# Gradient row operands made inside the last attention, dW2 stored there between zeros, and two-bank output tiles from the attention's end

## The chip, the cores and the metric

The kernel runs on one core of one Trainium2 chip. The metric is the device time of one execution in microseconds (us), lower is better. A time is quoted as the median of the runs of one kernel, with the lowest and highest in brackets. A profile is of one of those executions; its span is about 2 us shorter than the time of the same run. In the profile PE is the matmul engine, PEld its weight load, DVE, ACT and POOL the vector, scalar and general engines, SP the engine that here only issues transfers (SPq is its queue). L222 is a line of the kernel.

The program uses one core, so there is no second die to compare with. A run counts as slow when it is over 1.5% above the fastest of the same kernel.

## The reference, cut to what matters

One token goes through two identical layers (attention, then a Mish MLP) that share their weights, and the function returns the output and the gradients of everything.

```python
def _A_ref(x, k_cache, v_cache, wq, wo):      # D=1024, 32 query heads, 4 KV heads, Dh=128
    W = 4096                                  # a window at the end of a cache of Sk=32768
    q = (x @ wq).reshape(B, 1, 32, 128).transpose(0, 2, 1, 3)
    k = repeat(k_cache[:, :, Sk - W:], 8);  v = repeat(v_cache[:, :, Sk - W:], 8)
    p = softmax(einsum("bhqd,bhkd->bhqk", q, k) * Dh ** -0.5)
    return einsum("bhqk,bhkd->bhqd", p, v).reshape(B, 1, 4096) @ wo
def _B_ref(x, w1, b1, w2):                    # F=3584
    h = x @ w1 + b1
    return (h * tanh(softplus(h))) @ w2
def f(x, ...):
    x = x + _A_ref(_layernorm(x), ...); x = x + _B_ref(_layernorm(x), ...)
    x = x + _A_ref(_layernorm(x), ...); x = x + _B_ref(_layernorm(x), ...)
    return x
out, vjp = jax.vjp(f, x, k_cache, v_cache, wq, wo, w1, b1, w2)
return out, *vjp(grad_out)                    # y, dx, dK, dV, dWq, dWo, dW1, db1, dW2
```

Two things follow. The gradients of the shared weights are sums of two outer products, one per layer, so each is a matrix of rank 2: almost no arithmetic and much to store. And 7/8 of dK and dV are zeros, because only the window of the cache is read: 58.7 MB of zeros, stored as 112 transfers of 0.524 MB from one tile of zeros. These zero stores need no data, so the kernel may issue them at any time. They are the only work of which this is true. The profile gives 98.58 MB written to HBM and 72.89 MB read.

## The kernel before

The backward pass runs from the last layer to the first. The last big thing on it is the backward of the first layer's attention ("the last attention"): it streams wo in (the "wo stream"), forms the gradient of the softmax, multiplies by K, and then goes through the 32 heads with wq (the "dn loop", because it forms the gradient dn of the layer norm's output). After it come one layer norm and the outputs that are left: the last stage.

Zero stores are issued either from SP's queue (`zeros`) or from POOL's queue behind a small copy that waits for given data (`bg_zeros`). The table `Z` says how many at which point:

```python
def zeros(n):
    for _ in range(min(n, len(zero_jobs))):
        nc.sync.dma_start(zero_jobs.pop(0), zt[:])
def bg_zeros(n, after):
    if n:
        nc.gpsimd.tensor_copy(gate_t[:], after[:, 0:1])
    for _ in range(min(n, len(zero_jobs))):
        nc.gpsimd.dma_start(zero_jobs.pop(0), zt[:])
# A1c: at the start of the last attention.  A1d: in its middle.  end: behind its layer norm.
Z = dict(B2=3, A3=16, B4=[5, 2, 1, 2, 1, 2, 6], A3c=6, A3d=29, W1=3, A1c=6, A1d=26, end=4)
```

An output is a "job": four matmuls into PSUM, their evictions into a staging tile, one store of 0.524 MB (0.459 MB for dW1). A dK or dV job ("chunk") is stored only with its neighbours, after every fourth chunk; they are staged in the two halves of K's tile, which the prediction calls K halves. The operands of the matmuls are rows, made in "pieces": POOL copies columns into a tile of zeros, PE transposes eight blocks, one engine evicts.

```python
def spread_rows(n, put, dst):                       # one piece
    ...                                             # POOL: put() into a spread tile
    if "pair" in pools: ps = shaped(pools["pair"].tile([P, 2048], BF16, name="rw", tag="pair"), [P, 8, P])
    else:               ps = psum1([P, 8, P], BF16, "rw")
    for j in range(n):
        nc.tensor.transpose(ps[:, j, :], sp[:, j, :], ident_bf[:])
    evac(dst, ps[:, 0:n, :].rearrange("p j x -> p (j x)"), 0.69, 1.0)

def out_banks():                                    # PSUM for one job
    if "pair" in pools:                             # two tiles of two banks, 1024 columns an eviction
        ts = [pools["pair"].tile([P, 1024], FP32, name="ops", tag="pair") for _ in range(2)]
        return [t[:, k * 512:(k + 1) * 512] for t in ts for k in range(2)], [(0, 2, ts[0][:]), (2, 2, ts[1][:])]
    bs = [psum1([P, 512], FP32, "ops") for _ in range(4)]        # four tiles of one bank
    return bs, [(k, 1, bs[k]) for k in range(4)]
```

`psum1` takes one of only four one-bank buffers; the other four banks hold accumulators and, in the attention, two "halves" buffers. The end of the kernel, with cuts:

```python
# in the last attention
bg_zeros(Z["A1c"], g_bf)                            # the start, while the wo stream waits for its loads
...
zeros(Z["A1d"])                                     # behind the wo stream
...
after_v()                                           # V is read: its space becomes rows, spread and staging tiles
...
for h in range(HQ):                                 # the dn loop
    for half in range(2): row_mm(nrow, ...)         # 128*32 columns, 128x512 rows
    if h % 8 == 7: run(1)                           # one dW2 job every 8 heads (two more ran before the loop)
...
# after the last layer norm
bg_zeros(Z["end"], g0b)
rows_put(R["w1"], 0, "nB", "rep"); rows_put(R["w1"], 1, "dh", "pieces")
do3 = row_layout(...); do1 = row_layout(...); tall_left("wo", "o", 0); ...   # all other row operands
run(1000)                                           # 8 dW2 jobs and
dw_wide(lambda: R["w1"], 256, F // 2, True, out_6); run(4)       # 4 dW1 jobs in one-bank tiles
pools["pair"] = ...                                 # from here two-bank tiles
run(1000)                                           # 12 dW1
dkv(sA3["p"], do3, sA1["p"], do1, out_3); ...       # dV, dWo, dK, dWq
```

## Time and profile before

The time before is 459.68 us (458.19 to 460.98, 3 runs). The page's second part cuts the span into 40 slices of 11.5 us. The two rows shown are the busy share of the DMA engines in tenths and what they moved:

```profile
DMA  8999999988999999999998999999995889799997
GB/s 322 387 411 414 406 408 342 410 307 316 416 417 370 390 342 351 411 414 416 416 414 326 311 336 368 359 412 418 416 418 235 354 321 400 309 413 402 418 411 303
```

From slice 27 on (298 us and later) the DMA is the limit: slices at 412 to 418 GB/s, and a few below. The slices 31 to 35 are the ones below. Windows of 10 us show them better. Each row gives the window, its length, the busy time and count of each engine, the clock, the DMA share and GB/s:

```profile
core 0: us, PE busy (x) PEld busy (x) DVE busy (x) ACT busy (x) POOL busy (x), PEclk, DMA share, GB/s
300.00:310.00 10.00, 6.36 (x116) 4.34 (x108) 5.39 (x10) 6.36 (x7) 0.40 (x1) 0.96 1.02 411
330.00:340.00 10.00, 9.26 (x79) 2.14 (x77) 6.46 (x12) 3.01 (x6) 0.00 (x0) 0.58 1.03 417
350.00:360.00 10.00, 6.80 (x49) 4.19 (x47) 7.54 (x23) 4.36 (x6) 5.42 (x28) 0.50 0.63 253
360.00:370.00 10.00, 8.50 (x29) 1.73 (x26) 7.90 (x12) 8.50 (x15) 0.00 (x0) 0.50 0.82 329
370.00:380.00 10.00, 6.33 (x32) 1.31 (x31) 7.60 (x13) 8.46 (x11) 0.00 (x0) 0.50 0.80 319
390.00:400.00 10.00, 7.74 (x66) 2.12 (x62) 10.00 (x10) 9.46 (x10) 0.00 (x0) 0.84 0.73 292
```

A full window has a share of 1.02 or 1.03. The timeline (start, duration, engine, line, operation, output from inputs; in brackets how long the engine idled before it and for what) says what happens in the first low one:

```profile
346.51 0.17 DVE L309 CAST gX_pair<-g_A 128x8 bf16<-128x8 f32 x1
...
349.54 1.89 PE L887 MATMUL rw<-ident_bf,spread 128*128 128x128 bf16 x16 [1.75 <-POOL spread L897]
...
355.47 0.58 ACT L149 CAST wo_b<-ops 128x512 bf16<-128x512 f32 x1 [0.89 <-PE ops L223]
...
357.51 0.33 SPq L974 DMA_DIRECT2D out_dram<-wo_b  x1
```

The last layer norm ends at 346.5. Then the pieces are made, the first output is evicted at 355.5, and its store is issued at 357.5. The DMA lives on what was queued before and on four zeros.

In 300 to 310 the DMA is full although nothing is stored that was computed there. The DMA view of 300 to 304 us, by queue, says what fills it: the software queue, which here carries the six zeros of `A1c`.

```profile
q0 software_dynamic: 433, 1.59, 98.2%
q1 hardware_dynamic: 19, 0.05, 3.4%
```

To add such holes up I took windows of 1 us and summed `1 - share/1.025`, where positive, with 1.025 as the share of a full window. This gives 13.1 us of lost DMA time between 294 and 442 us. It is a sum worked out from the profile, and the rest of the document uses it.

### The profile page before, as it was taken

How to read it: one execution, taken by the hardware profiler on the slowest of the kernel's cores; microseconds unless marked ns; L12 is line 12 of the kernel's file. 1: busy time of each engine (PE TensorE's matmuls, PEld its weight loads, DVE VectorE, ACT ScalarE, POOL GpSimd, SP SyncE). 2: the span in 40 equal slices, each digit the busy share in tenths (PEclk: the TensorE clock that was granted, in tenths of full speed). 3: DMA queues.
4: the chain of work that ended last, by engine and by line, in shares of the span. 5: the costliest groups of instructions: out<-in, count | busy, mean ns of one | idle time of the engine just before them, and what ended most of it. 6: DMA issues, size and time to landing. Idle time of an engine off the chain costs nothing.

```text
span 458.9 us, 11945 instructions
## 1 busy us (share of the span) xinstructions
PE 328.7 (72%) x5080; PEld 225.6 (49%) x5080; DVE 246.9 (54%) x519; ACT 219.3 (48%) x268; POOL 61.5 (13%) x159
## 2 busy tenths in 40 slices
PE   0565755577996998877997889775885676779730
PEld 0333434566466997854895779643534111222100
DVE  3124101376332776663265755564555779999960
ACT  1122100165242886773581655351031689998940
POOL 2000000002422214142330020112006000000000
PEclk9989555596777999895697769987565555755555
DMA  8999999988999999999998999999995889799997
GB/s 322 387 411 414 406 408 342 410 307 316 416 417 370 390 342 351 411 414 416 416 414 326 311 336 368 359 412 418 416 418 235 354 321 400 309 413 402 418 411 303
DMA packets 52257, 172.24 MB, mean 375 GB/s; under 512 B 5200, under 2 KB 12396, under 8 KB 51180
## 3 DMA queue, kind: packets, MB, share of 16 engines
q1 hardware_dynamic: 39680, 126.37, 71.3%
q0 software_dynamic: 12480, 45.11, 24.5%
q8 instruction: 39, 0.64, 0.5%
q14 instruction: 14, 0.11, 0.1%
q10 hardware_dynamic: 44, 0.01, 0.0%
HBM read 72.89 MB, written 98.58 MB: 374 GB/s over the span
## 4 chain that ended last, share of the span: by engine, by line
PE 21%; issue 9%; DVE 8%; ACT 8%; DMA 7%; POOL 1%; DVEq 0%; ACTq 0%; SPq 0%; POOLq 0%
PE tps L187 6%; PE ops L223 5%; DMA w_c<-in_B_w_dram 4%; PE acc L223 4%; ACT wo_b L149 3%; DVE wq_b L146 3%; DMA wo_c<-in_A_wo_dram 3%; DVE K L146 3%; ACT st_o L149 2%; PE d L223 2%; PE tps L602 1%; PE sm L223 1%; PE rw L887 1%; ACT wo_c L149 1%; ACT w_c L603 1%
## 5 line engine op out<-in xcount | busy, mean ns | idle before, releaser
L139 POOL DMA_DIRECT2D out_dram<-zt x86 | 45.7, 535 | 43.3 <-DMA out_dram<-zt 40.7
L223 PEld LDWEIGHTS <-w_c 128*128 128x128 bf16 x1120 | 36.3, 102 | 20.9 <-DMA w_c<-in_B_w_dram 13.9
L603 ACT COPY w_c<-tps 128x1024 bf16<-128x1024 bf16 x28 | 28.3, 1012 | 25.5 <-PE tps L602 24.8
L146 DVE CAST wo_b<-ops 128x512 bf16<-128x512 f32 (+3 forms) x40 | 33.2, 878 | 9.2 <-PE ops L223 8.9
L605 DVE CUSTOM_DVE_ANT_0 scr<-w_c,gbc 128x1024 bf16<-128x1024 bf16 x28 | 34.2, 1221 | 7.2 <-DMA w_c<-in_B_w_dram 5.2
L149 ACT CAST wo_b<-ops 128x512 bf16<-128x512 f32 (+2 forms) x34 | 27.0, 870 | 16.4 <-PE ops L223 16.4
L149 ACT COPY K<-tps 128x1024 bf16<-128x1024 bf16 x19 | 18.7, 1019 | 30.9 <-PE tps L187 30.9
L223 PE MATMUL q<-wq_b,nA_pair 128*32 128x512 bf16 x128 | 14.0, 541 | 16.6 <-DMA wq_b<-in_A_wq_dram 15.1
L770 DVE CUSTOM_DVE_ANT_0 wo_c<-wo_c,gbc 128x1024 bf16<-128x1024 bf16 x14 | 16.3, 1218 | 12.4 <-DMA wo_c<-in_A_wo_dram 10.4
L602 PE MATMUL tps<-ident_bf,w_c 128*128 128x128 bf16 x224 | 22.7, 263 | 0.0
L146 DVE COPY K<-tps 128x1024 bf16<-128x1024 bf16 x13 | 8.8, 689 | 24.9 <-PE tps L187 24.9
L149 ACT COPY w_b<-tps 128x1024 bf16<-128x1024 bf16 x20 | 19.5, 1015 | 5.3 <-PE tps L187 5.2
L187 PE MATMUL tps<-ident_bf,K 128*128 128x128 bf16 x256 | 21.7, 249 | 0.0
L223 PE MATMUL ops<-Tw 2*128 2x512 bf16 x56 | 15.9, 560 | 6.5 <-ACT wo_b L149 4.1
L187 PEld LDWEIGHTS <-K 128*128 128x128 bf16 x256 | 18.4, 114 | 4.1 <-issue 4.0
L223 PE MATMUL acc<-a_pair,w_c 128*128 128x16 bf16 x448 | 16.0, 172 | 5.2 <-DMA w_c<-in_B_w_dram 4.2
L187 PE MATMUL tps<-ident_bf,w_c 128*128 128x128 bf16 x224 | 17.3, 238 | 1.6 <-DMA w_c<-in_B_w_dram 1.6
L146 DVE CAST K<-ops 128x1024 bf16<-128x1024 f32 x15 | 17.7, 1221 | 0.9 <-PE ops L223 0.6
L149 ACT CAST K<-ops 128x1024 bf16<-128x1024 f32 x17 | 17.0, 1012 | 1.7 <-PE ops L223 1.2
L149 ACT COPY w_c<-tps 128x768 bf16<-128x768 bf16 (+1 forms) x14 | 11.6, 829 | 12.6 <-PE tps L187 11.4
L149 ACT COPY wq_b<-tps 128x1024 bf16<-128x1024 bf16 x16 | 15.1, 1054 | 5.1 <-PE tps L187 5.1
L223 PE MATMUL ops<-R 2*128 2x512 bf16 (+1 forms) x64 | 12.3, 544 | 7.0 <-ACT wo_b L149 5.4
(333 smaller groups left out, 684.5 us busy)
## 6 DMA issues: line engine op xcount, KB each, us to landing
out_dram<-zt POOLq DMA_DIRECT2D x86, 512.0 KB, 10.0
wo_c<-in_A_wo_dram SPq DMA_DIRECT2D x28, 512.0 KB, 8.2
w_c<-in_B_w_dram SPq DMA_DIRECT2D x32, 448.0 KB, 5.9
w_c<-in_B_w_dram SPq DMA_DIRECT2D x28, 512.0 KB, 7.0
out_dram<-zt SPq DMA_DIRECT2D x26, 512.0 KB, 8.2
out_dram<-wo_b SPq DMA_DIRECT2D x18, 512.0 KB, 9.1
wq_b<-in_A_wq_dram SPq DMA_DIRECT2D x16, 512.0 KB, 11.8
out_dram<-K SPq DMA_DIRECT2D x8, 1024.0 KB, 8.4
```

The lines of the kernel that those rows point to most:

```text
L139: nc.gpsimd.dma_start(zero_jobs.pop(0), zt[:])
L146: nc.vector.tensor_copy(out_ap, in_ap)
L149: nc.scalar.copy(out_ap, in_ap)
L187: nc.tensor.transpose(ps[:, b, :], ap, ident_bf[:])
L223: nc.tensor.matmul(out_ap, lhsT=lhsT, rhs=rhs, start=start, stop=stop, skip_group_check=True, **kw)
L602: nc.tensor.transpose(ps[:, b, :], w[:, 1, b * P:(b + 1) * P], ident_bf[:])
L603: nc.scalar.copy(w[:, 1, :], ps[:].rearrange("p b c -> p (b c)"))
L605: nc.vector.tensor_tensor_reduce(out=scr[:], in0=w[:, 0, :], in1=gbc[:], scale=1.0, scalar=0.0, op0=ALU.mult, op1=ALU.add, accum_out=wg[:, ...
L770: nc.vector.tensor_tensor_reduce(out=w[:, 0, :], in0=w[:, 0, :], in1=gbc[:], scale=1.0, scalar=0.0, op0=ALU.mult, op1=ALU.add, accum_out=w ...
L887: nc.tensor.transpose(ps[:, j, :], sp[:, j, :], ident_bf[:])
```

## The change

It has three parts. (a) The row operands are made inside the last attention, in the space of wo (free once its rows have been used) and of V, so nothing has to be made after the layer norm. (b) All outputs after the attention use two-bank tiles. (c) dW2 jobs run inside the attention, each behind one zero store, ten in place of six; to have zeros for that, and for between the later outputs, 22 of the zeros that stood at the attention's start and middle are taken from there. The diff is shortened: some lines are joined, and the comments are added here.

```diff
@@ last attention, wo stream
+        if not first:
+            after_do()                              # spread tiles, T, R and staging inside wo_b; dW2 and dW1 jobs
+            prep.extend([...])      # dW2's left rows (2) and right rows, dW1's two sides, do3, q3, db1
         def T(i): ...
+            if not first and i: nextprep()          # one piece for each late wo chunk
@@ behind the wo stream
+            after_stream()
             zeros(Z["A1d"])
@@ softmax gradient
         else:
             after_v()
+            early(2)
-            tall_left("w2", "a", 0)
+            nextprep(1)
...
@@ dn loop
-            run(2)
+            prep.extend([...])      # 7 pieces: dWo's left rows (2) and right rows, dWq's two sides, do1, q1
         for h in range(HQ): ...
-            if not first and h % 8 == 7:
-                run(1)
+            if not first and h % 4 == 3:
+                nextprep()
+                early(1)
@@
+    def early(n):
+        for _ in range(n):
+            zeros(1)
+            run(1)
-    Z = dict(B2=3, A3=16, B4=[5, 2, 1, 2, 1, 2, 6], A3c=6, A3d=29, W1=3, A1c=6, A1d=26, end=4)
+    Z = dict(B2=3, A3=16, B4=[5, 2, 1, 2, 1, 2, 6], A3c=6, A3d=29, W1=3, A1c=0, A1d=10)
@@ last stage
-    R["w1"] = new_rows("R1"); rows_put(R["w1"], ...); do3 = row_layout(...) ...    # all pieces
-    bg_zeros(Z["end"], g0b)
     pacc.release()
-    run(1000)
-    dw_wide(lambda: R["w1"], 256, F // 2, True, out_6)
-    run(4)
     pt.release()
     pools["pair"] = ...
...
+    while jobs:
+        run(7)
+        zeros(1)
+    zeros(1000)
```

More of the change, by code (lines that the diff above doesn't have):

```diff
@@ L70 @@
     strm = ctx.enter_context(tc.tile_pool(name="strm", bufs=NB))
-    vpool = tc.alloc_tile_pool(name="vpool", bufs=1)
     pt = tc.alloc_tile_pool(name="pt", bufs=4, space=bass.MemoryType.PSUM)
@@ L374, in pipe @@
                 M(items[i - lag], i - lag)
+    area = {}
     def row_layout(col32, name):
-        x = pools["rows"].tile([P, G, DH], BF16, name=name, bufs=1)
+        x = area[name].rearrange("p (g d) -> p g d", g=G)
         ps = psum1([P, P], BF16, "rps")
@@ L381, in row_layout @@
             nc.vector.tensor_scalar(out=x[:, g, :], in0=ps[:, 0:P], scalar1=gmask[:, g:g + 1], scalar2=None, op0=ALU.mult)
-        return x
     def pad_tile(name):
@@ L426, in attn_fwd @@
                     nc.sync.dma_start(wq_t[2 * t + hf], wq_v[:, t, hf * (J // 2):(hf + 1) * (J // 2)])
-            load_kv(vpool, "V", v_v)
+            load_kv(keep, "V", v_v)
             for c in range(NR):
@@ L762, in attn_bwd @@
         nc.scalar.copy(de[:], drow[:])
+        if not first:
+            after_do()
+            prep.extend([
+                lambda: tall_left("w2", "a", 0),
+                lambda: tall_left("w2", "a", 1),
+                lambda: tall_right("w2", "gB"),
+                lambda: rows_put(area["R1"], 0, "nB", "rep"),
+                lambda: rows_put(area["R1"], 1, "dh", "pieces"),
+                lambda: row_layout(sA3["dorep"][:].rearrange("p c x -> p (c x)"), "do3"),
+                lambda: row_layout(sA3["qrep"][:].rearrange("p c x -> p (c x)"), "q3"),
+                db1_out,
+            ])
         def T(i):
@@ L782, in M @@
                 fill(1, ["V", "K", "wq"], "a")
+            if not first and i:
+                nextprep()
         pipe(list(range(len(late))), T, M)
@@ L828, in attn_bwd @@
         nc.vector.tensor_copy(sd[:], lps[:])
-        ds = keep.tile([P, WC], BF16, name="ds_A3") if first else pools["rows"].tile([P, WC], BF16, name="ds_A1")
+        ds = keep.tile([P, WC], BF16, name="ds_A3") if first else area["ds"]
         dsT = work.tile([P, TJ, P], BF16, name="dsT", tag="kp")
@@ L842, in attn_bwd @@
         if not first:
-            tall_left("w2", "a", 1)
+            nextprep(1)
         for hf in range(2):
@@ L850, in attn_bwd @@
         else:
-            tall_right("w2", "gB")
-            run(2)
+            nextprep(100)
+            prep.extend([
+                lambda: tall_left("wo", "o", 0),
+                lambda: tall_left("wo", "o", 1),
+                lambda: tall_right("wo", "gA"),
+                lambda: rows_put(area["Rq"], 0, "nA", "rep"),
+                lambda: rows_put(area["Rq"], 1, "dq", "heads"),
+                lambda: row_layout(sA1["dorep"][:].rearrange("p c x -> p (c x)"), "do1"),
+                lambda: row_layout(sA1["qrep"][:].rearrange("p c x -> p (c x)"), "q1"),
+            ])
         nrow = acc_tile(512)
@@ L857, in attn_bwd @@
                        wq_b[:, 4 * half:4 * half + 4, h // 16, (h % 16) * P:(h % 16 + 1) * P], h < 2, h >= HQ - 2)
-            if not first and h % 8 == 7:
-                run(1)
+            if not first and h % 4 == 3:
+                nextprep()
+                early(1)
         nps = sm_tile(P, TD)
@@ L870, in col_out @@
         nc.gpsimd.dma_start(out_flat.rearrange("(n p) -> n p", p=P), rt[0:n, :])
-    def new_rows(name):
-        return pools["rows"].tile([P, 2, 1024], BF16, name=name, tag="rows", bufs=1)
     def spread_rows(n, put, dst):
-        sp = pools["spread"][pools["sturn"] % 2]
+        sp = area["spread"][pools["sturn"] % 2]
         pools["sturn"] += 1
         for l in range(2):
-            put(sp[:].rearrange("p j (q x) -> p j q x", q=4), l)
-        if "pair" in pools:
-            ps = shaped(pools["pair"].tile([P, 2048], BF16, name="rw", tag="pair"), [P, 8, P])
-        else:
-            ps = psum1([P, 8, P], BF16, "rw")
+            put(sp.rearrange("p j (q x) -> p j q x", q=4), l)
+        ps = psum1([P, 8, P], BF16, "rw")
         for j in range(n):
@@ L911, in tall_left @@
     def tall_left(nm, kind, half):
-        if nm not in tall:
-            tall[nm] = pools["rows"].tile([P, 2560], BF16, name="T" + nm, bufs=1)
         src = pairs[kind]
@@ L1014, in dkv, with cut_up, after_do, after_stream @@
         jobs.extend([lambda j=j: chunk(j) for j in range(TJ)])
-    def after_v():
-        vpool.release()
-        rp = pools["rows"] = ctx.enter_context(tc.tile_pool(name="rows", bufs=1))
-        pools["spread"] = [rp.tile([P, 8, P], BF16, name=f"spread{i}") for i in range(2)]
-        pools["sturn"] = 0
-        for s in pools["spread"]:
-            nc.gpsimd.memset(s[:], 0.0)
-        slots.extend(wo_kept[c].rearrange("p t d -> p (t d)") for c in range(NR))
-        slots.extend(rp.tile([P, 2048], BF16, name=f"so{i}")[:] for i in range(2))
-        slots.extend(strm.tile([P, 2048], BF16, name="st_o", tag="st")[:] for _ in range(NB))
-        dw_tall("w2", TF, out_8.rearrange("(c p t) d -> c p t d", p=P, t=2))
-    Z = dict(B2=3, A3=16, B4=[5, 2, 1, 2, 1, 2, 6], A3c=6, A3d=29, W1=3, A1c=6, A1d=26, end=4)
+    wo_flat = wo_b[:].rearrange("p c t d -> p (c t d)")
+    def cut_up(flat, at, sizes):
+        out = []
+        for n in sizes:
+            out.append(flat[:, at:at + n])
+            at += n
+        return out
+    def after_do():
+        s0, s1, tall["w2"], area["do3"], area["q3"], _, r1 = cut_up(wo_flat, 0, (1024, 1024, 2560, 512, 512, 512, 2048))
+        area["spread"] = [s.rearrange("p (j x) -> p j x", x=P) for s in (s0, s1)]
+        area["R1"] = r1.rearrange("p (s x) -> p s x", s=2)
+        pools["sturn"] = 0
+        nc.gpsimd.memset(wo_flat[:, 0:2048], 0.0)
+        slots.extend(cut_up(wo_flat, 8192, (2048,) * (NR - 4)))
+        dw_tall("w2", TF, out_8.rearrange("(c p t) d -> c p t d", p=P, t=2))
+        dw_wide(lambda: area["R1"], 256, F // 2, True, out_6)
+    def after_stream():
+        slots.extend(strm.tile([P, 2048], BF16, name="st_o", tag="st")[:] for _ in range(NB))
+    def after_v():
+        vf = kv["V"][:].rearrange("p g t d -> p (g t d)")
+        tall["wo"], area["do1"], area["q1"], _, rq, area["ds"], _ = cut_up(vf, 0, (2560, 512, 512, 512, 2048, 1024, 1024))
+        area["Rq"] = rq.rearrange("p (s x) -> p s x", s=2)
+        slots.extend(cut_up(vf, 8192, (2048,) * 4))
+    prep = []
+    pz = [0]
+    def nextprep(n=1):
+        for _ in range(min(n, len(prep))):
+            prep.pop(0)()
+    def early(n):
[3 more added lines that the diff above has]
+    Z = dict(B2=3, A3=16, B4=[5, 2, 1, 2, 1, 2, 6], A3c=6, A3d=29, W1=3, A1c=0, A1d=10)
     x1 = None
@@ L1079, with db1_out @@
     g1, g1b = mlp_bwd_w1(g2, "B2", sB2, "A1")
+    def db1_out():
+        db1 = work.tile([P, 2, NW2], BF16, name="db1")
+        nc.vector.tensor_add(db1[:], sB4["dh"][:].rearrange("p (c t) -> p t c", t=2), sB2["dh"][:].rearrange("p (c t) -> p t c", t=2))
+        db_row = work.tile([NW2, P, 2], BF16, name="db_row", tag="kp", padded_shape=[NW2, WC // 2, 2])
+        for t in range(2):
+            dbps = psum1([NW2, P], BF16, "dbps")
+            nc.tensor.transpose(dbps[:], db1[:, t, :], ident_bf[:])
+            nc.vector.tensor_copy(db_row[:, :, t], dbps[:])
+        nc.gpsimd.dma_start(out_7.rearrange("(c x) -> c x", x=2 * P), db_row[:].rearrange("c p t -> c (p t)"))
@@ L1080 @@
     g0, g0b = attn_bwd(g1, g1b, "A1", sA1, False, "X0")
+    level()
+    nextprep(100)
     col_out(g0b, TD, out_1[0, 0, :])
-    level()
-    db1 = work.tile([P, 2, NW2], BF16, name="db1")
-    nc.vector.tensor_add(db1[:], sB4["dh"][:].rearrange("p (c t) -> p t c", t=2), sB2["dh"][:].rearrange("p (c t) -> p t c", t=2))
-    db_row = work.tile([NW2, P, 2], BF16, name="db_row", tag="kp", padded_shape=[NW2, WC // 2, 2])
-    for t in range(2):
-        dbps = psum1([NW2, P], BF16, "dbps")
-        nc.tensor.transpose(dbps[:], db1[:, t, :], ident_bf[:])
-        nc.vector.tensor_copy(db_row[:, :, t], dbps[:])
@@ L1090 @@
-    nc.gpsimd.dma_start(out_7.rearrange("(c x) -> c x", x=2 * P), db_row[:].rearrange("c p t -> c (p t)"))
-    R = {}
-    R["w1"] = new_rows("R1")
-    rows_put(R["w1"], 0, "nB", "rep")
-    rows_put(R["w1"], 1, "dh", "pieces")
-    do3 = row_layout(sA3["dorep"][:].rearrange("p c x -> p (c x)"), "do3x")
-    do1 = row_layout(sA1["dorep"][:].rearrange("p c x -> p (c x)"), "do1x")
-    tall_left("wo", "o", 0)
-    tall_left("wo", "o", 1)
-    tall_right("wo", "gA")
-    q3 = row_layout(sA3["qrep"][:].rearrange("p c x -> p (c x)"), "q3x")
@@ L1102, with r3 @@
-    q1 = row_layout(sA1["qrep"][:].rearrange("p c x -> p (c x)"), "q1x")
-    bg_zeros(Z["end"], g0b)
     top(None)
     pacc.release()
-    run(1000)
-    dw_wide(lambda: R["w1"], 256, F // 2, True, out_6)
-    run(4)
     pt.release()
     pools["pair"] = ctx.enter_context(tc.tile_pool(name="pair", bufs=4, space=bass.MemoryType.PSUM))
-    run(1000)
-    dkv(sA3["p"], do3, sA1["p"], do1, out_3)
-    run(1000)
+    def r3(nm):
+        return area[nm].rearrange("p (g d) -> p g d", g=G)
     slots.extend(wq_t)
+    dkv(sA3["p"], r3("do3"), sA1["p"], r3("do1"), out_3)
@@ L1115 @@
     dw_tall("wo", HQ, out_5.rearrange("(c p t) d -> c p t d", p=P, t=2))
-    run(4)
-    R["wq"] = new_rows("Rq")
-    rows_put(R["wq"], 0, "nA", "rep")
-    run(4)
-    rows_put(R["wq"], 1, "dq", "heads")
-    bg_zeros(1000, g0b)
-    run(1000)
-    dkv(sA3["ds"], q3, sA1["ds"], q1, out_2)
-    run(1000)
-    dw_wide(lambda: R["wq"], 512, 2048, False, out_4)
-    run(1000)
+    dkv(sA3["ds"], r3("q3"), sA1["ds"], r3("q1"), out_2)
+    dw_wide(lambda: area["Rq"], 512, 2048, False, out_4)
+    while jobs:
+        run(7)
+        zeros(1)
```

## The prediction

> **What bounds the kernel now.** The page: 172.24 MB at a mean of 375 GB/s over 458.9 us; full slices show about 417 GB/s. From 296 us (start of the last attention's backward) the windows add up to about 60.5 MB, which needs 145 us at 417 GB/s: an end near 442 us. So from there the kernel is DMA bound, plus about 16 us of holes and tail. The holes (10 us windows): 253 GB/s in 350-360, 329 and 319 in 360-380, 292 in 390-400. The timeline names them: in 346.5-354.6, after the last layer norm, all row operands are made while no output is evicted; then 12 outputs go through one-bank tiles, 1.75 us each, slower than the DMA takes them (0.524 MB / 417 GB/s = 1.26 us); then the first K half gives no store for 4 us.
>
> **What the change does.** Bytes are unchanged. (a) Operand making moves inside the attention: 6 pieces in the wo stream, 2 by the softmax gradient, 7 in the dn loop. (b) All outputs after the attention use two-bank tiles: 1.22 us (DVE) and 1.02 us (ACT) per 1024 columns, so 1.0-1.15 us a tile, faster than DMA. (c) 10 dW2 jobs inside in place of 6, each with a zero store. (d) Zero stores: 6 at the attention's start become 0, 26 in its middle 10, 10 go between the jobs, 16 into the last stage.
>
> **Cost on the critical path.** What the DMA lacks counts, not engine work.
> - Gain: the holes of 354-400 us, about 2.1+2.3+0.2+3.0 = 7.6 us, and 8 us of operand making.
> - New hole 1: in 300-304 us 98% of the traffic is the software queue's, which is just those 6 zeros; the seventh wo load is issued at 303.8. Without them about 5.5 us idle.
> - The stream becomes DVE bound (five evictions, masks) and ends about 1 us later. Two dW2 jobs put 7 one-bank evictions of 0.61 us before the softmax gradient: +4 us. Before spent 3 us on two jobs later, so the dn loop starts at about 331.5 us, as before (331.25).
> - Hole 2: the middle zeros (11 in a row) end at about 320.6 us, first dW2 data 322.7: 2 us. Hole 3: two stores and two zeros last until 328; the next store comes from the dn loop at 335-337: 8 us.
> - The dn loop took 10 us with 4 jobs; now 8 jobs and 7 pieces, about 2.2-2.8 us a round: 18-22 us. Hole 4 at its end, 2-5 us (layer norm, release of the banks, first wide eviction).
> - The last stage's first store moves data at about 360 us; 43.0 MB remain (34.6 outputs, 16 zeros), 104 us at 412 GB/s.
>
> The clock matters little: the Trainium skill, "TensorE: Matmul & The Clock Gate", Part 1, says the clock halves without recent activity; the trace agrees (0.50 in 350-390 us).
>
> **Prediction:** 465 us, 457 to 473. The last stage becomes clean, but holes inside the attention give back more than was won. Faster by 2%: 0.04; within 2%: 0.70; slower: 0.26.
>
> **What would show it.** Windows: 300-305 us under half busy; 328-336 nearly idle; last stage at 410 GB/s throughout, no dip at the first K half; first wide eviction at 357-362 us. Timeline: dn loop 18-22 us against 10.
>
> **What would make it wrong.** Well overlapped evictions could make a round 1.7 us, then the end falls near 455. The seventh load could land early enough to move the attention 3 us forward. Or banks (four one-bank tiles shared by jobs and pieces) stall the loop to over 3 us a round: then over 470.

## The result, and the profile after

After: 476.71 us (476.02 to 478.68, 4 runs). Before, on the same chip: 460.33 us (458.19 to 462.94, 4 runs). The ratio is 1.036, with a 95% interval of 1.030 to 1.042. A ratio here is the mean time of one kernel's fast runs over that of the other's of the same rounds, so not quite the ratio of the medians. The change makes the kernel 3.6% slower. The spans of the two profiles are 458.9 and 474.2 us, with mean clocks of 0.720 and 0.706.

The same two rows of the page, after (slices of 11.9 us):

```profile
DMA  8999999999999999999998999394583999999997
GB/s 324 384 415 419 406 400 358 360 334 377 416 391 377 336 361 377 404 416 417 415 417 334 361 345 366 135 401 183 208 325 158 406 402 408 414 412 420 417 410 319
```

The last stage is clean: 402 to 420 GB/s over slices 32 to 39, where before, in the same slices, had 309 to 418. But in front of it four slices between 296 and 368 us are at 135 to 208 GB/s; before has one below 300 there, at 235. The windows:

```profile
300.00:310.00 10.00, 8.07 (x155) 7.01 (x151) 6.09 (x11) 7.56 (x8) 5.12 (x23) 0.96 0.62 223
...
320.00:330.00 10.00, 6.18 (x118) 4.53 (x117) 6.21 (x17) 1.17 (x2) 0.00 (x0) 0.57 0.53 217
330.00:340.00 10.00, 8.48 (x85) 3.30 (x82) 3.77 (x7) 2.83 (x6) 2.76 (x15) 0.50 0.27 107
340.00:350.00 10.00, 8.85 (x58) 2.51 (x57) 4.76 (x9) 4.90 (x8) 0.65 (x4) 0.50 0.78 316
...
360.00:370.00 10.00, 5.93 (x34) 2.41 (x35) 6.85 (x13) 5.33 (x6) 0.52 (x1) 0.50 0.39 156
370.00:380.00 10.00, 5.63 (x36) 0.96 (x32) 8.43 (x9) 9.32 (x9) 0.00 (x0) 0.50 1.01 405
...
390.00:400.00 10.00, 9.01 (x62) 1.94 (x55) 9.06 (x8) 9.57 (x11) 0.00 (x0) 0.50 1.00 403
```

The stretch 300 to 310 went from 411 to 223 GB/s and 330 to 340 from 417 to 107. From 370 us on the trouble is gone: 405 where before had 319, and 403 where it had 292. What the DMA waits for is in the timeline of SP's queue. After the store and the zero of 322 us nothing is issued for 13 us, because the next store in this in-order queue needs the first dW2 job of the dn loop, and the zeros of the later rounds stand behind it:

```profile
322.31 0.33 SPq L991 DMA_DIRECT2D out_dram<-wo_b  x1
322.68 0.64 SPq L129 DMA_DIRECT2D out_dram<-zt  x1
336.14 0.33 SPq L991 DMA_DIRECT2D out_dram<-wo_b  x1
```

PE's own timeline shows the dn loop: in each round 8 matmuls of the loop (acc), a piece (8 transposes, rw), a dW2 job (four ops):

```profile
341.35 1.04 PE L222 MATMUL acc<-wq_b,dq_pair 128*32 128x512 bf16 x8
342.32 1.03 PE L906 MATMUL rw<-ident_bf,wo_b 128*128 128x128 bf16 x8
343.29 0.61 PE L222 MATMUL ops<-wo_b 2*128 2x512 bf16 x3
344.14 0.58 PE L222 MATMUL ops<-wo_b 2*128 2x512 bf16 x1 [0.24 <-DVE V L145]
344.65 1.05 PE L222 MATMUL acc<-wq_b,dq_pair 128*32 128x512 bf16 x8
...
347.98 0.58 PE L222 MATMUL ops<-wo_b 2*128 2x512 bf16 x1 [0.77 <-DVE st_o L145]
```

A round takes 3.3 us (341.35 to 344.65), at a clock of 0.50. The piece and the job take five tiles from four one-bank buffers, so the job's fourth tile cannot start with the other three: it starts 0.85 us after them (344.14 against 343.29), when the piece has been evicted. PE itself idles for 0.24 to 0.77 us of a round. The loop runs from 331.15 to 358.40 us, 27.3 us, where before ran from 331.25 to 341.74. From its end to the first output of the last stage (DVE and ACT in the timeline):

```profile
358.40 0.68 DVE L238 COPY yr<-acc 128x512 f32<-128x512 f32 x1
...
364.67 1.01 ACT L148 CAST st_o<-ops 128x1024 bf16<-128x1024 f32 x1 [7.06 <-PE ops L222]
```

The lost DMA time by stretch, summed as above (us; worked out from the windows of 1 us), for the two kernels and for the experiments that follow:

| kernel | 294-310 | 310-326 | 326-340 | 340-358 | 358-368 | 368-380 | 380-400 | 400-442 | sum | span | span less sum |
|---|---|---|---|---|---|---|---|---|---|---|---|
| before | 0.3 | 0.2 | 0.1 | 5.0 | 1.7 | 2.4 | 3.0 | 0.3 | 13.1 | 458.9 | 445.8 |
| after | 7.6 | 1.6 | 11.0 | 3.4 | 6.9 | 0.3 | 0.4 | 0.3 | 31.5 | 474.2 | 442.7 |
| a1 | 0.8 | 0.1 | 0.1 | 6.5 | 7.4 | 0.8 | 0.6 | 0.4 | 16.6 | 461.1 | 444.5 |
| a2 | 7.8 | 3.4 | 10.2 | 14.1 | 4.1 | 0.1 | 0.1 | 0.4 | 40.2 | 487.2 | 447.0 |
| a3 | 0.5 | 0.2 | 0.1 | 7.3 | 0.2 | 0.1 | 2.4 | 0.3 | 11.1 | 457.0 | 445.9 |
| a4 | 6.6 | 1.2 | 8.5 | 0.3 | 1.7 | 0.6 | 3.7 | 0.3 | 22.8 | 470.6 | 447.8 |
| b1 | 0.3 | 0.2 | 0.2 | 0.3 | 0.5 | 2.3 | 4.6 | 0.4 | 8.8 | 452.7 | 443.9 |
| d1 | 6.2 | 1.3 | 10.5 | 0.6 | 1.2 | 0.1 | 0.3 | 0.3 | 20.6 | 466.4 | 445.8 |
| d2 | 7.9 | 1.7 | 10.5 | 5.1 | 5.1 | 0.2 | 0.4 | 0.3 | 31.3 | 474.4 | 443.1 |
| c1 | 0.5 | 0.2 | 0.1 | 2.6 | 1.0 | 0.1 | 3.7 | 0.4 | 8.5 | 452.8 | 444.3 |
| c2 | 0.4 | 0.2 | 0.1 | 1.2 | 0.2 | 0.5 | 3.7 | 0.3 | 6.6 | 449.3 | 442.7 |
| e1 | 0.3 | 0.9 | 10.6 | 3.8 | 6.8 | 0.2 | 0.4 | 0.3 | 23.4 | 467.0 | 443.6 |
| e2 | 6.3 | 1.5 | 10.5 | 3.4 | 5.5 | 3.2 | 2.8 | 3.9 | 37.1 | 484.1 | 447.0 |

The sums differ by 18.4 us between before and after, the spans by 15.3. Part of the rest is that after is earlier at its start of this stretch: it had moved 112.63 MB when 296 us had passed, before 111.34; the 1.3 MB are 3 us at 0.42 MB/us. The texts below were written with edges placed by eye at each hole, so their holes differ from this table by a few tenths (10.5 for the third and 3.9 for the fourth, for example).

### The profile page after: what moved, and what is told of

It is laid out like the page before. It is cut to its first block, busy times and chain, and to the rows that moved or that the text cites. A ratio compares the mean times of both kernels' runs of the same rounds, so it can differ in the third digit from the quotient of the medians.

```text
span 474.2 us, 11910 instructions
## 1 busy us (share of the span) xinstructions
PE 329.4 (69%) x5080; PEld 222.8 (47%) x5080; DVE 244.8 (52%) x510; ACT 218.0 (46%) x261; POOL 56.1 (12%) x145
## 4 chain that ended last, share of the span: by engine, by line
PE 23%; ACT 10%; issue 7%; DMA 7%; DVE 4%; POOL 0%; DVEq 0%; ACTq 0%; SPq 0%; POOLq 0%
PE ops L222 6%; PE tps L186 6%; PE acc L222 5%; DMA w_c<-in_B_w_dram 4%; ACT wq_b L148 3%; ACT st_o L148 2%; PE sm L222 2%; DMA wo_c<-in_A_wo_dram 2%; PE tps L602 1%; ACT K L148 1%; DMA out_dram<-V 1%; ACT V L148 1%; PE rw L906 1%; ACT wo_b L148 1%; ACT wo_c L148 1%
## 5 line engine op out<-in xcount | busy, mean ns | idle before, releaser
L222 PE MATMUL ops<-V 2*128 2x512 bf16 (+1 forms) x160 | 34.4, 599 | 5.9 <-ACT st_o L148 1.7
L222 PE MATMUL ops<-wo_b 2*128 2x512 bf16 x120 | 25.5, 562 | 15.5 <-ACT st_o L148 5.9
L222 PEld LDWEIGHTS <-V 128*128 128x128 bf16 (+2 forms) x416 | 14.1, 101 | 27.8 <-issue 27.6
L148 ACT CAST st_o<-ops 128x1024 bf16<-128x1024 f32 (+2 forms) x22 | 18.4, 901 | 15.0 <-PE ops L222 15.0
L148 ACT CAST wq_b<-ops 128x1024 bf16<-128x1024 f32 (+1 forms) x24 | 23.7, 1066 | 1.8 <-PE ops L222 1.4
L145 DVE CAST st_o<-ops 128x512 bf16<-128x512 f32 (+2 forms) x22 | 20.0, 940 | 6.2 <-PE ops L222 6.2
L145 DVE CAST wq_b<-ops 128x1024 bf16<-128x1024 f32 (+1 forms) x20 | 22.5, 1188 | 1.1 <-PE ops L222 0.9
L602 PE MATMUL tps<-ident_bf,w_c 128*128 128x128 bf16 x224 | 22.7, 263 | 0.0
L145 DVE CAST wo_b<-ops 128x512 bf16<-128x512 f32 (+2 forms) x22 | 18.5, 880 | 6.0 <-PE ops L222 5.4
L148 ACT CAST wo_b<-ops 128x1024 bf16<-128x1024 f32 (+1 forms) x18 | 15.1, 937 | 12.5 <-PE ops L222 12.4
L782 DVE CUSTOM_DVE_ANT_0 wo_c<-wo_c,gbc 128x1024 bf16<-128x1024 bf16 x14 | 16.6, 1216 | 6.7 <-DMA wo_c<-in_A_wo_dram 4.6
```

Source lines behind the costliest of these rows:

```text
L145: nc.vector.tensor_copy(out_ap, in_ap)
L148: nc.scalar.copy(out_ap, in_ap)
L222: nc.tensor.matmul(out_ap, lhsT=lhsT, rhs=rhs, start=start, stop=stop, skip_group_check=True, **kw)
L602: nc.tensor.transpose(ps[:, b, :], w[:, 1, b * P:(b + 1) * P], ident_bf[:])
L782: nc.vector.tensor_tensor_reduce(out=w[:, 0, :], in0=w[:, 0, :], in1=gbc[:], scale=1.0, scalar=0.0, op0=ALU.mult, op1=ALU.add, accum_out=w ...
```

## The experiments

Two theories stood against each other. Theory S (starved): from 296 us on the time is bytes over rate plus the time in which the DMA has nothing to move; the 22 zeros that the change took away had covered stretches in which nothing else can be stored. Rival C (chain): the last stage starts later (364.67 against 355.47 us for the first eviction), because pieces and jobs lengthen the dn loop, and this delay of 9 us of computation sets the end.

### a1: the changed kernel with the zeros where they were

```diff
-    Z = dict(..., A1c=0, A1d=10)
+    Z = dict(..., A1c=6, A1d=26)
     def early(n):
         for _ in range(n):
-            zeros(1)
             run(1)
```

This takes 10 zeros out of the attention's jobs and 12 out of the last stage, and puts them at the front.

> The changed kernel with the zero stores where the kernel before had them (6 at the attention's start, 26 in its middle, none between the jobs, 4 left for the end). Theory S (starved): from 296 us the time is bytes over rate plus the holes in the DMA; the zeros now fill 297-304 and 326-336, about 43 stores of 1.26 us from 300 us, so holes of 31 us shrink to about 13 and the time falls to about 459 us (455 to 463). Rival C (chain): the attention's own chain, 18 us longer by pieces and jobs inside it, sets the end; then the time stays at 474 us or more.

Measured: 463.94 us (463.07 to 466.80), ratio to before 1.010 (1.004 to 1.016; before 459.5 us on this chip).

```profile
330.00:340.00 10.00, 8.46 (x142) 4.67 (x139) 2.60 (x6) 2.03 (x5) 2.77 (x15) 0.50 1.03 416
...
360.00:370.00 10.00, 5.82 (x29) 3.06 (x30) 5.94 (x13) 3.47 (x4) 0.52 (x1) 0.50 0.27 106
```

```profile
366.53 1.01 ACT L148 CAST st_o<-ops 128x1024 bf16<-128x1024 f32 x1 [7.04 <-PE ops L222]
```

The first eviction of the last stage comes at 366.53 us, 1.9 us later than in after, and the kernel is about 2.5% faster (1.0101 against 1.036, each over before). C said that a later chain ends later; it falls. The window 330 to 340 is full again. The time lies just above the expected 455 to 463, since the holes sum to 16.6 us and not to 13. What stays is the hole of 340 to 368 us, 13.9 us: the front zeros have run out before the long loop and the layer norm are over. And the kernel is still 1.0% slower than before: with the zeros in their old places, all the rest of the change together gains nothing yet.

### a2: the kernel before with the zeros of the change

```diff
-    Z = dict(..., A1c=6, A1d=26, end=4)
+    Z = dict(..., A1c=0, A1d=10, end=0)
...
-    run(1000)                 # in the last stage, at each place
+    while jobs: run(3); zeros(1)
```

> The kernel before with the zero counts of the changed one (0 at the start, 10 in the middle, 26 spread over the last stage), nothing else changed. Theory S: 17 stores of 1.26 us are all there is to do between 300 and 357 us, so about 36 us of holes there in place of 5, and the last stage's 7 us of holes mostly filled: 484 us (476 to 490). Rival C: the chain is untouched, so 456 to 463 us.

Measured: 486.53 us (484.97 to 489.45), ratio 1.059 (1.052 to 1.065).

```profile
350.00:360.00 10.00, 5.82 (x46) 4.42 (x47) 6.95 (x24) 3.78 (x5) 5.04 (x30) 0.67 0.01 3
```

While the operands are made, 3 GB/s move where before moved 253. Nothing of the computation was changed, only where 26 zeros stand (the change's 22 and the four of `end`), and it costs 27 us (486.53 against 459.5). With a1 this settles that the place of the zeros is the first cause. It also shows that parts (a) and (b) are worth something: under the same poor placing of zeros the changed kernel has 31.5 us of holes and this one 40.2.

### a3: the kernel before with two-bank tiles for all outputs

```diff
     pacc.release()
+    pt.release()
+    pools["pair"] = ctx.enter_context(tc.tile_pool(name="pair", bufs=4, ...))
     run(1000)
     dw_wide(lambda: R["w1"], 256, F // 2, True, out_6)
     run(4)
-    pt.release()
-    pools["pair"] = ...
```

> The kernel before with only the two-bank tiles for the 8 dW2 and the first dW1 outputs after the attention (part b of the change alone). Theory S: removes the holes of 360-380 us and most of that at 390-400, so 4 to 6 us faster: 454 to 457 us. Rival C says about the same size, since it shortens the chain as well; this run sizes part b only.

Measured: 457.6 us (455.55 to 458.77), ratio 0.995 (0.989 to 1.0003). The holes of 358 to 380 us went from 4.1 us to 0.3, as expected; the one of 340 to 358 grew from 5.0 to 7.3. Two us are left of four (454 to 457 us were expected), and the interval just includes no change. The trace shows that the growth is there before the edit's place, which is behind the layer norm. In a3 the dn loop, whose code is the same, starts 1.2 us later (332.45 us), and the clock stays at 0.50 through it where it rose in before. So it ends at 344.56 us, 2.8 us later than before's 341.74, and the four zeros that end the hole are issued 2.8 us later too (355.64 against 352.83). In a2, with the same loop again, the clock rose in its last round: in this loop the clock differs between executions.

### a4: the changed kernel with the loop's seven pieces made in the last stage

```diff
         if not first and h % 4 == 3:
-                nextprep()
                 early(1)
...
-    nextprep(100)
...
     slots.extend(wq_t)
+    for k in range(7):
+        run(2)
+        nextprep()            # its PSUM from the pair pool
+        if k % 3 == 2: zeros(1)
```

> The changed kernel with the seven operand pieces of the dn loop made in the last stage between outputs (where engines have 30 us to spare), zeros as in the changed kernel. Both theories: the loop's rounds fall from 3.3 to about 2.6 us, first store of the last stage about 5 us sooner. Theory S: the loop's store and zero then come more densely, same bytes, so about 5 us faster: 471 us (469 to 474).

Measured: 470.97 us (467.16 to 472.58), ratio 1.022 (1.014 to 1.030). Without pieces the loop takes 15.1 us (335.03 to 350.09), 12 us less than in after, and the kernel gains about 6. The holes of 340 to 368 go from 10.3 to 2.0 us, but the stretch 368 to 400 loses 4.3 where after lost 0.7: the pieces now stand in the stage that has to feed the DMA. Off the chain is not free either; it costs less. One more thing is seen here:

```profile
336.00:348.00 12.00, 12.00 (x88) 2.03 (x84) 7.77 (x13) 7.54 (x15) 0.13 (x1) 0.50 0.78 317
```

PE is busy for all of these 12 us, as the profile counts it, and the clock stays at 0.50. Idle time of PE is therefore not what holds the clock down here.

### e1: only the six zeros of the start

```diff
-    Z = dict(..., A1c=0, A1d=10)
+    Z = dict(..., A1c=6, A1d=10)
```

> The changed kernel with only the 6 zero stores at the attention's start put back (taken from the 16 of the last stage). Theory S: the hole of 7.4 us at 297-304 closes, the last stage has 6 stores fewer, the chain moves 1 to 2 us later because the seventh wo load shares the DMA: 5 to 7 us faster than the changed kernel, 471 us (468 to 473). If the zeros only delay the seventh load, it is as slow or slower: 477 us.

Measured: 468.57 us (467.51 to 473.99), ratio 1.020 (1.014 to 1.025).

```profile
300.00:310.00 10.00, 8.04 (x146) 6.77 (x142) 5.81 (x13) 7.20 (x8) 5.12 (x23) 0.94 1.01 400
```

The first hole closes from 7.6 to 0.3 us, all others stay (10.6, 3.8, 6.8), and the kernel gains 8 us between medians, of different chips. Six zeros are 3.1 MB, 7.5 us at 0.42 MB/us: put where nothing else can be stored they were worth their whole length, and taken from the last stage, where the DMA was full anyway, they cost nothing.

### e2: the changed kernel with one-bank tiles for the first 20 outputs

```diff
     pacc.release()
+    for n in (7, 7, 6):
+        run(n)
+        zeros(1)
     pt.release()
     pools["pair"] = ...
```

> The changed kernel with one-bank tiles for the first 20 outputs after the attention (4 dW2, 16 dW1), undoing part b where it stands. Theory S: such an output takes 1.5 to 1.75 us where the DMA needs 1.1 to 1.26, so 8 to 12 us of small holes less three zeros of 1.26 us: 483 us (479 to 488). If the last stage has engine time to spare without harm (its evictions end 30 us before the DMA), 477 us.

Measured: 484.49 us (483.99 to 485.92), ratio 1.052 (1.048 to 1.056).

```profile
380.00:390.00 10.00, 7.28 (x26) 1.57 (x26) 6.54 (x13) 8.04 (x13) 0.00 (x0) 0.50 0.85 336
```

Over 368 to 442 us the holes are 9.9 us where after has 1.0, and the kernel is about 7.5 us slower (1.0523 against 1.036, times 460). Two-bank tiles for all outputs are a true gain, as the prediction had them. (In before's timeline of 357 to 360 us PE waits 0.64 to 0.67 us for an eviction ahead of every pair of one-bank matmuls.)

### d1: the loop's pieces in banks of their own

Why is a round 3.3 us and not 2.2 to 2.8? Two causes were open: jobs and pieces share four one-bank buffers, and the clock is half. d1 gives the pieces of the loop the two "halves" buffers, which are free by then; d2 leaves the banks and raises the clock.

```diff
-        ps = psum1([P, 8, P], BF16, "rw")
+        if pools.get("h"): ps = shaped(pools["top"].tile([P, 1024], BF16, name="rw", tag="h"), [P, 8, P])
+        else:              ps = psum1([P, 8, P], BF16, "rw")
...
+                pools["h"] = True
                 nextprep()
+                pools["h"] = False
                 early(1)
```

The tiles of the two single transposes of the last pieces (`rps`) move in the same way.

> The changed kernel, only the seven pieces in the dn loop take their result tiles from the two banks that the softmax gradient has left, so the dW2 jobs keep the four one-bank tiles to themselves. If bank waits made the rounds long (3.3 us against 1.8 without pieces), they fall to about 2.9 us, the piece's own matmul time of 1.04 us at the half clock staying: loop 23 us, time 473 us (470 to 475). If banks don't matter, 476 to 477 us.

Measured: 467.91 us (467.09 to 472.66), ratio 1.018 (1.009 to 1.026); better than expected.

```profile
335.36 0.61 PE L222 MATMUL ops<-wo_b 2*128 2x512 bf16 x4
...
337.85 0.61 PE L222 MATMUL ops<-wo_b 2*128 2x512 bf16 x4
...
340.74 0.62 PE L914 MATMUL rw<-ident_bf,wo_b 128*128 128x128 bf16 x8
...
342.31 0.62 PE L914 MATMUL rw<-ident_bf,wo_b 128*128 128x128 bf16 x8
```

The four ops of a job now run in one go. At the same half clock a round is 2.49 us (335.36 to 337.85) in place of 3.3. And then, at about 339.7 us, something happens that I had not expected: eight transposes go from 1.03 to 0.62 us, so the clock has risen, without anything done for it, and rounds take 1.57 us (340.74 to 342.31). The mean clock of 340 to 350 us is 0.81 where after had 0.50. The loop takes 18.0 us (332.59 to 350.58), the holes of 340 to 368 fall from 10.3 to 1.8 us, and the total is where the prediction had put it. The Trainium skill, "TensorE: Matmul & The Clock Gate", section "A second HAM failure mode: psum-queue depth-cycling", describes a link of this kind: small idles of PE between groups of matmuls, from cycling PSUM buffers, make the clock go down and up again and again. That this is the cause here is not shown. The idles were taken away and the clock rose, in d1 and also in c1 (only at about 345.9 us; its loop takes 20.0 us) and c2 (18.2 us); but in after the clock did not go up and down, it stayed at 0.50, and in a4, and in b1 below, the same idles are gone and it stays at 0.50 too. Why it rose in d1 is open. What d1 shows without the clock is the 2.49 us.

### d2: dense matmuls in every round

```diff
                 nextprep()
                 early(1)
+                dum = pools["top"].tile([P, 512], FP32, name="dum", tag="h")
+                for k in range(4):
+                    mm(dum[:], ident_bf[:], wq_b[:, k, 0, 0:512], True, True)
```

Nobody reads their result; the outputs are those of the changed kernel.

> The changed kernel with four dense matmuls (128x128 by 512 columns, result never read) added to every round of the dn loop. [...] If they bring the clock up, the other matmuls of the round halve (2.7 to 1.4 us) and the round stays near 3.3 us or falls to 2.8; the clock row then shows 1.0 in 335-360 us. If the clock stays at 0.5, the round grows to about 5 us and the time to about 488 us.

Measured: 478.02 us (476.14 to 481.47), ratio 1.040 (1.030 to 1.050), so no gain over after.

```profile
344.23 0.61 PE L222 MATMUL acc<-wq_b,dq_pair 128*32 128x512 bf16 x8
...
346.18 0.37 PE L222 MATMUL ops<-wo_b 2*128 2x512 bf16 x1 [0.46 <-DVE V L145]
346.48 1.04 PE L222 MATMUL dum<-wq_b,ident_bf 128*128 128x512 bf16 x4
347.45 0.61 PE L222 MATMUL acc<-wq_b,dq_pair 128*32 128x512 bf16 x8
```

The clock is 1.00 over 340 to 360 us, and the loop's eight matmuls take 0.61 us in place of 1.04. But the round is still 3.22 us (344.23 to 347.45): the four dense matmuls themselves take 1.04, and the fourth ops tile still waits 0.46. Without the dense ones this is about 2.2 us, which is arithmetic and not a run. So the shared banks are worth 0.8 us of the 3.3 (d1, at the same clock), and the half clock about 1 us by this estimate, which no run shows as a gain.

### b1 and b2: all together with late pieces

b1 is a1 and a4 together, with the last four zeros put behind the loop's last store (`zeros(4)` after the `for h` loop). b2 is b1 with the dV chunks mixed among the dWo jobs and the dK chunks among the dWq jobs, one to two.

```diff
+        if not first:
+            zeros(4)                       # b1: behind the dn loop
...
+    def mixed(wide_jobs, kv_jobs): ...     # b2: jobs in the order wide, wide, chunk
-    dkv(sA3["p"], ...); dw_tall("wo", ...)
+    mixed(lambda: dw_tall("wo", ...), lambda: dkv(sA3["p"], ...))
```

> The changed kernel with both repairs: zeros in front as the kernel before had them (6 and 26), the last 4 right behind the loop's last store, and the seven loop pieces made in the last stage. Theory S: about 47 stores and loads of 1.26 us are queued from 300 us, which covers the stretch to the last stage's first store at about 358 us nearly without a hole; then 34.6 MB at 412 GB/s and the hole of about 3 us at the first K half: 448 us (444 to 452). If the two repairs merely overlapped (each already has what the other gives), it would be near 459 us.

> As b1, but the chunks of the K and V gradients are spread between the dwo and dwq outputs (two outputs, one chunk), so that stores never pause for four chunks. Theory S: takes away the hole at the first K half, 2 to 4 us faster than b1: 445 us (442 to 449). If the K half's hole was only a symptom of an empty queue that b1 has filled, it is the same as b1.

Measured, b1: 456.28 us (455.47 to 460.40), ratio 0.992 (0.984 to 1.0003; one of the seven runs of before was slow). There is hardly a hole until 368 us (1.5 us in all), and then 6.9 us in 368 to 400. b2: the two fast runs took 451.45 and 454.69 us, two more were slow (458.74 and 459.01); ratio of the fast runs 0.983 (0.972 to 0.995). Both missed what was expected, 444 to 452 and 442 to 449 us.

### c1 and c2: front zeros, own banks

c2 is the changed kernel with the zeros at the front as in a1, the loop's pieces in their own banks as in d1, and `zeros(4)` behind the loop. c1 is c2 with the mixing of b2.

> Zeros in front (6, 26, 4 behind the loop), the seven loop pieces kept in the loop but in their own two banks, and the K and V chunks spread between other outputs. Theory S: the loop ends near 350 us, the queue holds until the last stage's first store at about 358-360 us, and the last stage makes nothing but outputs from its start: holes from 296 us under 5 us, against 12.6 in the kernel before: 0.975 of the kernel before (0.965 to 0.985), 447 us if that runs 459.

> As c1 without spreading the K and V chunks. Theory S: a hole of 3 to 4 us at the first K half is left: 0.982 of the kernel before (0.972 to 0.99). If c1 and c2 are the same, spreading the chunks is worth nothing.

Measured, c2: 453.3 us (450.17 to 456.67), ratio 0.984 (0.979 to 0.989). c1: 453.63 us (450.13 to 456.47), ratio 0.984 (0.980 to 0.989). Before took 461.0 us on this chip (11 runs, two of them slow). Both beat both kernels: 1.6% faster than before, with an interval that excludes no change and does not reach 2%, and 5% faster than after (0.984 against 1.036). In c2:

```profile
350.00:360.00 10.00, 6.07 (x33) 3.18 (x34) 5.93 (x13) 4.02 (x5) 0.52 (x1) 0.50 0.91 367
...
380.00:390.00 10.00, 9.16 (x64) 2.13 (x64) 9.07 (x8) 9.34 (x11) 0.00 (x0) 0.50 0.66 269
```

The stretch of the layer norm loses 1.2 us in place of 5.0. What remains is 3.7 us in 380 to 400, where a half of dV is held back until its fourth chunk. Mixing the chunks with other jobs (c1) does not remove it: 3.7 us as well. In the kernels with zeros between the later jobs (after, a1, d1, e1) this stretch loses only 0.3 to 0.6 us. It looks as if one or two zeros there would close it, but in c2 all are spent by then, and a variant with a zero held back for this place was not run.

## Why the prediction was wrong

The prediction was 465 us with a range of 457 to 473, and the time was 476.71. The direction and the mechanism were right: it said that the last stage becomes clean and that holes inside the attention give back more than was won. The size was off by 11.7 us, which left the range and the class that it thought likeliest, within 2%. Point by point, with the table's stretches:

- **"From there the kernel is DMA bound."** Right, and the table's last column shows how far: in 13 kernels, from 449 to 487 us, the span less the lost DMA time is 442.7 to 447.8 us (b2, whose profile is a slow one, is left out). The rate of after's slices 32 to 39, 402 to 420 GB/s, is near the 425 GB/s that the Trainium skill, "DMA: Bandwidth & Descriptors", section "Measured", gives for 16 MB loaded by one core alone; here most of it is stores.
- **Gain, "7.6 us, and 8 us of operand making".** The last stage, 368 to 442 us, loses 1.0 us where before lost 5.7. The gains are real (e2 shows it for the tiles), but there was no more to win than all of before's holes, 13.1 us; the prediction's 15.6 us were too many by 2.5. Its 8 us are the time in which the engines made operands; the DMA, which still had stores queued, lost only 5.0 us there (340 to 358). In its sum the new holes, 17.5 to 20.5 us, then left a net loss of 2 to 5; measured are 31.5 less 13.1, or 18.4, of which an earlier start gave 3 back; that this start about offsets the overstated gain is luck.
- **Hole 1, "about 5.5 us idle".** 7.6 us. Right in place and cause (e1), short in size.
- **Hole 2, "2 us".** 1.6 us. Right.
- **Hole 3, "8 us".** 11.0 us. The queue was empty at about 326 us and not at 328, and the next store was issued at 336.14, inside the predicted 335 to 337. "328-336 nearly idle" was right: the window 330 to 340 moved 107 GB/s.
- **"The dn loop starts at about 331.5 us, as before."** 331.15 us. Right.
- **"About 2.2-2.8 us a round: 18-22 us."** This is the step that failed: the cost of a round had no wait for PSUM buffers in it. A round took 3.3 us and the loop 27.3 us, because the piece and the job of a round share four one-bank buffers. The prediction had named this, but only as what would make it wrong: "banks ... stall the loop to over 3 us a round: then over 470". With banks of its own a round took 2.49 us at the same clock of 0.50 (d1), inside the predicted 2.2 to 2.8. With the longer loop came a hole inside it, 3.4 us, that was not in the sum, since a loop of 20 us would have fed the DMA: eight zeros and eight dW2 jobs are 8.4 MB, 20 us at 0.42 MB/us. d1 changes only the banks of the loop's pieces; its loop takes 18.0 us and its time is 467.91 us, inside the range. So the loop's length accounts for some 8 to 9 of the 11.7 us (1.036 less 1.018, times 460, or the difference of the medians). A part of this is the clock, which rose in d1's loop by itself.
- **"The clock matters little."** Not settled. At half clock the loop's eight matmuls take 1.04 us in place of 0.61 and eight transposes 1.03 in place of 0.62 (d2, d1), so the clock is a term of a round's cost in a loop where PE is busy for 8.5 to 8.9 us of 10 (330 to 350 us). But d1's 2.49 us at half clock shows that the predicted round did not need the full one, and d2, at 1.00, gained nothing. The prediction cited the Trainium skill, "TensorE: Matmul & The Clock Gate", Part 1, for a clock that is half by default and released by sustained activity, and it took the 0.50 of before's 350 to 390 us for agreement. The traces agree in the two levels, 0.50 and 1.00. They do not show want of activity as the reason: PE was busy for 27.88 of those 40 us, and in a4 for 12.00 of 12 us, at 0.50. The trace of before already showed both the clock and the wait for a bank, in a loop with half the jobs and no pieces: 16 of its matmuls took 1.90 us at the start (clock 0.50 over 331 to 337 us) and 1.05 at the end (1.00 over 339 to 341), and the fourth one-bank tile of a job waited 0.70 us:

```profile
331.25 1.90 PE L223 MATMUL acc<-wq_b,dq_pair 128*32 128x512 bf16 x16
...
334.39 0.58 PE L223 MATMUL ops<-Tw 2*128 2x512 bf16 x1 [0.70 <-ACT wo_b L149]
...
339.10 1.05 PE L223 MATMUL acc<-wq_b,dq_pair 128*32 128x512 bf16 x16
```

- **Hole 4, "2-5 us".** 6.9 us. From the loop's end to the first eviction are 6.3 us (358.40 to 364.67). Before's trace had most of it: from the same copy to the end of its layer norm are 4.8 us (341.74 to 346.51). The loop's slow supply adds to this hole too, since nothing is queued when the loop ends; in d1 the whole stretch 340 to 368 loses 1.8 us.
- **"First wide eviction at 357-362 us."** 364.67 us; 356.85 in d1. This is again the loop.
- **"Last stage at 410 GB/s throughout, no dip at the first K half."** Right: 402 to 420 GB/s, and 403 in 390 to 400, where before had 292.

What caused the slowdown as such is shown by a1, a2 and e1: 22 zeros moved from stretches in which nothing else can be stored to stretches that were full, or would have been. That the longer loop also needs more cover than before is shown by a1 (13.9 us lost in 340 to 368 with the zeros at the front); in c2, which adds d1's banks and the four zeros behind the loop, that falls to 1.4 us. Open remain what raises the clock in the dn loop, and whether the 3.7 us at the held-back half can be removed from c2.

## What to carry to other kernels

In a kernel bound by stores, the stores that need no data are a budget: spend them where nothing else can be stored, and count the lost DMA time of each stretch before moving one, since a zero in a full stretch buys nothing and a zero taken from an empty one costs its whole length. Moving work in under the DMA pays only if the queue stays fed meanwhile, so cost each round of such a loop with the clock and the PSUM buffers that it will really have, from a stretch of the trace in the same state. Work that is put between a loop's matmuls should get PSUM banks of its own: here this alone took a round from 3.3 to 2.5 us at the same clock; it was 1.6 where the clock rose, for a reason that stays open.

## What the Trainium skill lacked or had wrong

- "TensorE: Matmul & The Clock Gate", section "Why this matters for your kernels", says to keep TensorE busy for at least 4 us without a break to reach the full clock. Busy as the profile counts it is not enough: in a4 PE was busy 12.00 of 12.00 us (336 to 348), with no idle time in its timeline, and the clock stayed at 0.50; b1 shows the same over 334 to 346. Four dense matmuls of 128x512 in a round brought it to 1.00 with PE busy 8.35 of 10 (d2, 340 to 350). Matmuls of 2 rows or of 32 columns, of which a4's loop consists, seem to count for less, which no run here isolates.
- The same page, Part 1, puts the cost of the clock's ramp at under 1% of a typical kernel; it speaks of the warm-up. In this kernel of small matmuls the half clock is not only a warm-up: the changed kernel's mean clock was 0.706, and in the dn loop the rounds went from 2.49 to 1.57 us with the clock (d1).
- "DMA: Bandwidth & Descriptors" gives rates and latencies, but neither this page nor any other that I read says how to keep a queue fed through a stretch without data. Here the placing of 26 transfers of 0.524 MB was worth 27 us in the kernel before (a2), and that of 22 about 12 us in the changed one (a1, 1.010 against 1.036).
